# Decay attention and a softplus MLP on one core: another operation for the weights' sign, chunk 1's attention events one slot later, and the last weight sums spread over three steps

## The chip, the cores and the metric

The kernel runs on one core of one Trainium2 chip. The metric is device time in microseconds (us) of one execution. TensorE (PE in the profile) does the matmuls, VectorE (DVE), ScalarE (ACT) and GpSimd (POOL) the elementwise work, and SyncE (SP) issues most transfers; ACT issues some.

## The reference

The inputs are q, k, v of shape 4 x 8 x 768 x 64 (batch, heads, positions, dims), a decay per head, and two weight matrices `w_in` (512 x 2048) and `w_out` (2048 x 512), which come as float64. Cut to what matters:

```python
for b in range(nb):                      # 12 blocks of 64 positions
    intra = einsum('bhic,bhjc->bhij', qb, kb) * Dmask        # lam ** (i - j), causal
    out[block] = einsum('bhij,bhjd->bhid', intra, vb) + einsum('bhid,bhde->bhie', qb * lam_pow, kv_state)
    kv_state = lam ** 64 * kv_state + einsum('bhsd,bhse->bhde', kb * rev_pow, vb)
x = out as (4 * 768, 512)
h = x @ w_in
g = maximum(h, 0) + log1p(exp(-abs(h)))  # softplus
return (g @ w_out).astype(float32)
```

## The kernel before

**Chunks, units, slots.** The 768 positions are six chunks of 128. In each chunk the eight heads form four pairs, so there are 24 attention *units* g = 4 x chunk + pair. The MLP works on one chunk of all four batches at a time: 512 columns of x, 16 slices f of the hidden layer. Chunks 0 and 1 (`STD = 2`) take one *slot* s per slice, s = 4 to 31: `mlp1(s)` makes h in 12 matmuls, `chain_act`, `chain_hi`, `chain_lo` (named after their slot) make softplus and its two parts, and `mlp2(s)`, four slots later (`LAG`), adds 12 matmuls to the four output banks. Every value is split in a high and a low part in TensorE's number format, and three of the four products are taken. Chunks 2 to 5 go in two groups of two by a Strassen-like scheme with seven block products P1 to P7 per pair of slices (`product`); there a *step* i does two slices. The loop over steps stands once for chunks 2 and 3 (`more` true) and once for chunks 4 and 5.

**Weights.** `wts` holds the raw words of the float64 weights. `w_scale` (ACT) scales the high word as if it were a float, into `c`; `w_round` (ACT) rounds the low word to its top three bits, in place; `w_shift` (DVE) shifts `c` left by 3; `w_sign` (DVE) puts in the sign; `w_add` (DVE, an exact integer add) adds the low word; `w_hi` (ACT) and `w_lo` (DVE) split the result. In the first slots this goes block by block in an order written out by hand; from slot 4 on a group of two blocks is loaded into one tile `raws`, scaled, shifted and added in one slot (`new`) and split in the next (`old`). The converted blocks are written to DRAM (`store_blocks`) and read back later (`load_w1`, `load_w2`). `block_sums`, `store_sums` and `send_sums` make the block sums that the scheme needs, split them (a copy on ACT, then a subtraction on DVE) and send them to DRAM; sums 0 to 6 are made in slots 18 to 31, sums 7 in the steps.

**Attention beside the MLP.** Unit g needs `k_decay` (ACT), `q_decay` (DVE), scores (`mm_scores`, into banks x and y), `mask_scores` and `update_states` (DVE), and a slot later or more `mm_out`, whose result is copied to `xr` (`x_raw`). `event(g)` does `mm_out` of unit g - 1, then scores, mask, copy and states of unit g. `both_at` says in which slot each event stands; `k_decay` and `q_decay` are issued at the start of the slot before (`units_at`). Events 9 to 16 lie in slots 16, 18, ..., 30, between two `mlp2` of one slot; the slot after has no `mlp2`. Units 17 and up have their event in the steps. In the last slots `x_sums_early` and `x_sums_late` prepare the inputs of P1 to P7 from `xr`: the early ones of half 0 in slot 29, the late ones of half 0 in slot 30, the early ones of half 1 in slot 31, the late ones of half 1 behind it, just ahead of the steps.

**Order and storage.** Each engine works in program order (`manual_schedule`). A transfer waits in SP's queue until its buffer is free, and those behind it wait too. Large tiles share 21 buffers (`t8`), conversion and g tiles seven (`t4`), attention tiles five (`t2`). Of the eight PSUM banks four hold outputs (`obank`), two are the work tile `t` (`work`), and two (`bank`) are taken in turn by h, by the scores x and y of an event, and in the steps by a and c.

Of the kernel before, what the change touches and what calls it, by code (L numbers as in the profile page):

```python
# [7 lines left out]
F32 = mybir.dt.float32  # L8
F32R = mybir.dt.float32r
U32 = mybir.dt.uint32  # L10
AF = mybir.ActivationFunctionType
ALU = mybir.AluOpType
PSUM = bass.MemoryType.PSUM
# [5 lines left out]
NP = H // 2  # L19
# [3 lines left out]
NF = DFF // 128  # L23
LAG = 4
# [8 lines left out]
def decay_attention_softplus_ffn(  # L33
# [7 lines left out]
    nc = tc.nc  # L41
# [168 lines left out]
    def raw_at(ks, word):  # L210
        i = ks[0] % 2
        return raws[ks[0]][:, i : i + len(ks), :, word]
# [12 lines left out]
        nc.vector.tensor_single_scalar(out=c, in_=c, scalar=3, op=ALU.logical_shift_left)  # L225

    def w_sign(*ks):
        c = conv[ks[0]]
        nc.vector.scalar_tensor_tensor(  # L229
            out=c, in0=raw_at(ks, 1), scalar=0x80000000, in1=c, op0=ALU.bitwise_and, op1=ALU.bitwise_or  # L230
        )

    def w_add(*ks):
# [196 lines left out]
    def mlp2(ss):  # L430
        c = ss[0] // NF
        ends = ss[-1] % NF == NF - 1
        if ss[0] % NF == 0:
            o_tiles[c] = [obank(f"o{c}_{b}") for b in range(B)]
        if ends:
            ob = t8([128, B, 512], F32, f"ob{c}")
        for b in range(B):
            for s in ss:
                f = s % NF
                g, w = g_tiles[s], w_second(s)  # L440
                for n, (i, j) in enumerate(((0, 0), (0, 1), (1, 0))):
                    nc.tensor.matmul(  # L442
                        o_tiles[c][b], lhsT=g[:, i, b * 128 : (b + 1) * 128], rhs=w[:, j],
                        start=f == 0 and n == 0, stop=f == NF - 1 and n == 2,
                    )
            if ends:
                copy = nc.vector.tensor_copy if b % 2 else nc.scalar.copy
                copy(out=ob[:, b], in_=o_tiles[c][b])
                queue = nc.scalar if c == NCH - 1 and b % 2 == 0 else nc.sync
                queue.dma_start(out=out[b * S + c * C : b * S + (c + 1) * C, :], in_=ob[:, b])  # L450
# [147 lines left out]
    def low_of(g, l):  # L598
        nc.vector.tensor_sub(out=g[:, 1], in0=l, in1=g[:, 0])  # L599
# [37 lines left out]
    last = STD * NF  # L637
    scores_at = {3 * n + 3: NP + n for n in range(NP)}
    outs_at = {s + 2: g for s, g in scores_at.items()}
    scores_at[NF - 1] = 2 * NP  # L640
    both_at = {2 * g - 2: g for g in range(2 * NP + 1, 4 * NP + 1)}
    units_at = {**scores_at, **both_at}

    def event(g):
# [12 lines left out]
    for s in range(LAG, last):  # L657
        if s + 1 in units_at:
            k_decay(units_at[s + 1])
            q_decay(units_at[s + 1])  # L660
        chain_act(s - 1)
        chain_hi(s - 1)
        chain_lo(s - 1)
        old, new = w_group(s - 1), w_group(s)
        if old:
            w_hi(*old)
        if new:
            w_scale(*new)
            w_round(*new)
        if old:  # L670
            w_lo(*old)
        if new:
            w_shift(*new)
            w_sign(*new)
            w_add(*new)
        if s - 1 not in both_at:
            mlp2([s - LAG])
        if s in scores_at:
            scores_of(scores_at[s])
            if scores_at[s] == 2 * NP:  # L680
                keep_values(2 * NP)
        if s in both_at:
            event(both_at[s])
            mlp2([s + 1 - LAG])
        if s in outs_at:
            g = outs_at[s]
            w = work(f"z{g}")
            mm_out(g, w)
            x_high(g, w)
            x_low(g, w)  # L690
        mlp1(s)
        w_load(2 * s + (8 if s < 9 else 6))
        if s in units_at and s < NF - 2:
            load_upto(units_at[s] + 2)
        if s >= NF - 2 and s % 2 == 0:
            load_upto(2 * NP + 2 + (s - NF + 2) // 2 + (s >= NF))
        if s > NF and s % 2 == 0:
            load_w2((s - NF) // 2)
        if s > NF + 2 and s % 2 == 0:
            send_sums((s - NF) // 2 - 2)  # L700
        if 8 <= s < 8 + NF:
            store_blocks(s - 8)
        if s > NF and s % 2 == 0:
            block_sums((s - NF) // 2 - 1)
        if s > NF + 2 and s % 2:
            store_sums((s - NF - 1) // 2 - 1)
        for at, name, n in ((23, "P1", 0), (23, "P1", 1), (25, "P2", 0), (25, "P2", 1)):
            if s == at:
                x_block(name, xr[2][:, n + (2 if name == "P2" else 0)], n)
        if s == last - 3:  # L710
            x_sums_early(2, 0)
        if s == last - 2:
            x_sums_late(2, 0)
            load_w1(0)
        if s == last - 1:
            x_sums_early(2, 1)
# [14 lines left out]
    for c in range(STD, NCH, 2):  # L731
        more = c + 2 < NCH
        lb = {}
        gs = {}
        for i in range(NF // 2):
            if more and i == 1:
                block_sums(NF // 2 - 1)
                store_sums(NF // 2 - 1)
                send_sums(NF // 2 - 1)
            unit = nxt if more else None  # L740
            if unit is not None:
                load_upto(unit + 2)
            if i + 1 < NF // 2:
                load_w1(i + 1)
            load_w2(i)
            if unit is not None and unit < NG:
                k_decay(unit)
                q_decay(unit)
            if i % 2 == 0:
                l4 = t8([128, 4, 512], F32, f"lb{c}_{i}")  # L750
            for n in range(2):
                lb[2 * i + n] = l4[:, 2 * (i % 2) + n]
            ta, tb = t4([128, 2, 512], F32, f"ta{c}_{i}"), t4([128, 2, 512], F32, f"tb{c}_{i}")
            p1, u2, u3, c21 = ta[:, 0], ta[:, 1], tb[:, 0], tb[:, 1]
            a, b_ = bank(f"a{c}_{i}"), work(f"b{c}_{i}")[:, 0]
            product("P1", i, a)
            nc.scalar.copy(out=p1, in_=a)  # L757
            product("P6", i, b_)
            nc.vector.tensor_add(out=u2, in0=b_, in1=p1)  # L759
            c_ = bank(f"c{c}_{i}")  # L760
            product("P5", i, c_)
            product("P2", i, a, False)
            la = tl([128, 512], F32, f"la{c}_{i}")
            nc.scalar.activation(la, a, AF.Softplus)  # L764
            ga = parts_of(f"g{c}_{2 * i}", la)
            product("P7", i, b_, False)
            nc.vector.tensor_add(out=u3, in0=b_, in1=p1)  # L767
            nc.vector.tensor_add(out=u3, in0=c_, in1=u3)
            nc.scalar.activation(lb[2 * i + 1], u3, AF.Softplus)
            low_of(ga, la)  # L770
            run(rest, 2)
            product("P4", i, b_, False)
            nc.vector.tensor_add(out=c21, in0=b_, in1=p1)
            nc.scalar.activation(c21, c21, AF.Softplus)
            gb = parts_of(f"g{c}_{2 * i + 1}", c21)
            product("P3", i, c_, False)
            nc.vector.tensor_add(out=u2, in0=c_, in1=u2)
            nc.scalar.activation(lb[2 * i], u2, AF.Softplus)
            run(rest, 4)
            if unit is not None and unit <= NG:  # L780
                event(unit)
                nxt += 1
            low_of(gb, c21)
            run(rest)
            pair = [(2 * i + n, (ga, gb)[n], w2_tiles[i][:, n]) for n in range(2)]
            rest = seconds(c, pair, i == NF // 2 - 1)
        ahead = 2
        def split(f):
            gs[f] = parts_of(f"g{c + 1}_{f}", lb[f])
            low_of(gs[f], lb[f])  # L790
        for f in range(ahead):
            split(f)
        for i in range(2):
            load_w2(i)
        run(rest)
        xc.clear()
        steps = []
        if more:
            steps = [lambda n=n, m=m: x_block(n, xr[c + 2][:, m + (2 if n == "P2" else 0)], m) for n in ("P1", "P2") for m in range(2)]
            for n in range(2):  # L800
                steps += [lambda n=n: x_sums_early(c + 2, n), lambda n=n: x_sums_late(c + 2, n)]
        for f in range(NF - 2):
            if f % 2 == 0 and f // 2 + 2 < NF // 2:
                load_w2(f // 2 + 2)
            if f + ahead < NF:
                split(f + ahead)
            if f >= 1:
                run(steps, 1)
            if f == 9 and more:
                load_w1(0)  # L810
            run(seconds(c + 1, [(f, gs.pop(f), w2_tiles[f // 2][:, f % 2])]))
        rest = seconds(c + 1, [(f, gs[f], w2_tiles[f // 2][:, f % 2]) for f in (NF - 2, NF - 1)], True)
# [41 lines left out]
```

## Time and profile before

| | |
|---|---|
| time, median of 3 | 597.03 us (596.62 to 598.16) |
| profiled execution, time | 595.9 us |
| profiled execution, span | 594.1 us |
| PE busy | 576.5 us, 97% of the span |
| DVE busy | 321.6 us, 54% |
| ACT busy | 256.8 us, 43% |
| granted TensorE clock | 0.999 |

A row of the views by line gives line, engine, operation, the tiles written and read, count, then busy time, mean ns of one, and the idle time of the engine just ahead. A row of the timeline gives start, duration, engine, line, operation, and in brackets the idle time ahead and what ended it. A row of the view by stretches gives the busy time of PE, PE's weight loads, DVE, ACT and POOL, each with its number of instructions, the granted clock, the busy share of the DMA engines and the GB/s.

### The profile page before, as it was taken

The numbers are of one execution on the slowest core, as the hardware profiler recorded it, in microseconds if no ns is written. First come the engines' busy times: TensorE is split into PE (matmuls) and PEld (weight loads), VectorE is DVE, ScalarE is ACT, GpSimd is POOL, SyncE is SP. The second block draws the span as 40 slices with busy tenths as digits, with TensorE's granted clock in tenths as the row PEclk, the third lists the DMA queues.
The fourth block names the chain that finished last, engine by engine and source line by source line (L and its number), as shares of the span: only waits on it lengthen the run. The fifth ranks groups of instructions, "written<-read, shape, count | busy, mean of one in ns | idle before, by whom it ended". The sixth has DMA issues, their size and how long they took to land.

```text
span 594.1 us, 12014 instructions
## 1 busy us (share of the span) xinstructions
PE 576.5 (97%) x5203; PEld 469.4 (79%) x5203; DVE 321.6 (54%) x492; ACT 256.8 (43%) x416; POOL 4.1 (1%) x11
## 2 busy tenths in 40 slices
PE   8899989989999999989999999999999999999997
PEld 6677778768888888778888888888888888888886
DVE  7779998974767768664543443295133333333410
ACT  3777776663345434543333332463142222224310
POOL 2000000000000000000000000000000000000000
PEclk9999999999999999999999999999999999999999
DMA  8997565883999974649965647489267454473101
GB/s 292 407 407 272 186 202 178 273 298 114 327 399 387 412 285 172 253 159 386 413 257 188 237 171 271 155 315 375 88 237 294 167 190 140 137 288 121 56 1 71
DMA packets 38452, 142.34 MB, mean 240 GB/s; under 512 B 3712, under 2 KB 5760, under 8 KB 31360
## 3 DMA queue, kind: packets, MB, share of 16 engines
q1 hardware_dynamic: 35808, 136.86, 62.7%
q10 hardware_dynamic: 2592, 4.72, 2.1%
q8 instruction: 41, 0.67, 0.5%
q14 instruction: 11, 0.09, 0.0%
HBM read 112.20 MB, written 29.36 MB: 238 GB/s over the span
## 4 chain that ended last, share of the span: by engine, by line
PE 76%; DVE 10%; DMA 8%; ACT 2%; issue 1%; SPq 1%; DVEq 0%; ACTq 0%
PE o L607 30%; PE b L588 11%; PE h L421 8%; PE o L442 8%; PE c L588 7%; PE a L588 7%; DMA att<-in_att 4%; DMA g<-w 3%; PE x L311 2%; PE z L326 2%; DVE c L235 2%; DVE st L343 2%; DMA raw<-in_wts 1%; DVE w L242 1%; DVE c L229 1%
## 5 line engine op out<-in xcount | busy, mean ns | idle before, releaser
L607 PE MATMUL o<-w,g 128*128 128x512 f32 x816 | 192.7, 390 | 0.0
L607 PEld LDWEIGHTS o<-w,g 128*128 128x128 f32 x816 | 152.5, 188 | 31.9
L421 PE MATMUL h<-x,w 128*128 128x512 f32 x384 | 94.4, 395 | 2.1 <-DVE w L242 2.1
L421 PEld LDWEIGHTS h<-x,w 128*128 128x128 f32 x384 | 70.9, 188 | 19.9 <-DVE w L242 3.7
L442 PE MATMUL o<-w,g 128*128 128x512 f32 x336 | 82.3, 393 | 1.1 <-DVE w L242 0.8
L442 PEld LDWEIGHTS o<-w,g 128*128 128x128 f32 x336 | 62.3, 188 | 15.1 <-DVE w L242 1.2
L588 PE MATMUL a<-xcP,w1a 128*128 128x512 f32 x192 | 49.0, 391 | 1.5 <-ACT ta L757 1.5
L588 PE MATMUL b<-xcP,w1b 128*128 128x512 f32 x192 | 48.8, 389 | 0.0
L759 DVE TENSOR_TENSOR ta<-b,ta 128x512 f32<-128x512 f32 x16 | 11.0, 690 | 60.9 <-PE b L588 60.9
L588 PEld LDWEIGHTS a<-xcP,w1a 128*128 128x128 f32 x192 | 35.9, 188 | 9.8 <-ACT ta L757 2.3
L588 PEld LDWEIGHTS b<-xcP,w1b 128*128 128x128 f32 x192 | 36.0, 188 | 7.5
L402 ACT ACTIVATE l<-h 128x512 f32<-128x512 f32 x32 | 19.0, 595 | 49.1 <-PE h L421 46.5
L599 DVE TENSOR_TENSOR g<-lb,g 128x512 fp32r<-128x512 f32 x32 | 21.1, 688 | 34.1 <-ACT g L595 34.1
L767 DVE TENSOR_TENSOR tb<-b,ta 128x512 f32<-128x512 f32 x16 | 11.1, 691 | 50.4 <-PE b L588 50.4
L338 DVE TENSOR_TENSOR a<-x,mask 128x512 f32<-128x512 f32 x15 | 10.4, 691 | 44.1 <-PE y L313 23.4
L410 DVE TENSOR_TENSOR g<-l,g 128x512 fp32r<-128x512 f32 x32 | 22.1, 690 | 18.8 <-ACT g L406 18.7
L764 ACT ACTIVATE la<-a 128x512 f32<-128x512 f32 x16 | 9.6, 598 | 52.3 <-PE a L588 52.3
L757 ACT COPY ta<-a 128x512 f32<-128x512 f32 x16 | 9.3, 584 | 51.8 <-PE a L588 51.8
L595 ACT CAST g<-lb 128x512 fp32r<-128x512 f32 x32 | 18.7, 619 | 18.4 <-PE o L607 17.6
L588 PE MATMUL b<-xcP,w1a 128*128 128x512 f32 x96 | 24.9, 391 | 0.8 <-DVE xcP L561 0.4
L326 PEld LDWEIGHTS z<-qd,st 64*64 64x64 f32 x640 | 17.0, 134 | 10.0 <-issue 9.7
L386 ACT COPY xr<-z 128x512 f32<-128x512 f32 x16 | 9.4, 585 | 36.0 <-PE z L330 35.5
(100 smaller groups left out, 774.4 us busy)
## 6 DMA issues: line engine op xcount, KB each, us to landing
w<-g SPq DMA_DIRECT2D x39, 1024.0 KB, 5.6
att<-in_att SPq DMA_DIRECT2D x48, 512.0 KB, 10.0
raw<-in_wts SPq DMA_DIRECT2D x32, 512.0 KB, 10.2
w1a<-g SPq DMA_DIRECT2D x16, 1024.0 KB, 6.8
g<-w SPq DMA_DIRECT2D x24, 512.0 KB, 9.3
w1b<-g SPq DMA_DIRECT2D x16, 768.0 KB, 6.7
g<-parts SPq DMA_DIRECT2D x16, 512.0 KB, 9.0
out_dram<-ob ACTq DMA_DIRECT2D x18, 256.0 KB, 2.0
```

Source lines behind the costliest of these rows:

```text
L235: nc.vector.tensor_add(out=c, in0=c, in1=raw_at(ks, 0))
L311: nc.tensor.matmul(x[r, cols], lhsT=k[r, b, t], rhs=q[r, b, t], start=True, stop=True)
L326: nc.tensor.matmul(w[half(t), s, cols], lhsT=st[r, b, t], rhs=qd[r, b, t], start=True, stop=False)
L343: nc.vector.scalar_tensor_tensor(out=to[:, :, t], in0=of[:, :, t], scalar=lam_c[r, h : h + 1], in1=u[:, :, t], op0=ALU.mult, op1=ALU.add,)
L402: nc.scalar.activation(l_tiles[s], h_tiles.pop(s), AF.Softplus)
L410: nc.vector.tensor_sub(out=g[:, 1, :], in0=l_tiles.pop(s), in1=g[:, 0, :])
L421: nc.tensor.matmul(h_tiles[s], lhsT=w[:, i, cs], rhs=x[:, j, :], start=p == 0 and n == 0, stop=p == NP - 1 and n == 2,)
L442: nc.tensor.matmul(o_tiles[c][b], lhsT=g[:, i, b * 128 : (b + 1) * 128], rhs=w[:, j], start=f == 0 and n == 0, stop=f == NF - 1 and n == 2,)
L588: nc.tensor.matmul(to, lhsT=w[:, k, n, p * 128 : (p + 1) * 128], rhs=x[:, j, p], start=start and p == 0 and m == 0, stop=p == 1 and m == 2 ...
L595: nc.scalar.copy(out=g[:, 0], in_=l)
L599: nc.vector.tensor_sub(out=g[:, 1], in0=l, in1=g[:, 0])
L607: nc.tensor.matmul(outs[c, b], lhsT=g[:, i, b * 128 : (b + 1) * 128], rhs=w[:, j], start=f == 0 and n == 0, stop=f == NF - 1 and n == 2,)
```

## The change

Three places. `w_sign` no longer masks the sign out of the raw high word and joins it to `c`; it takes the 16-bit half that holds the sign, masks it, and writes it over the upper half of the rounded low word of the same tile, so that the add that follows brings it in. Events 9 to 16 move to slots 17, 19, ..., 31, with `k_decay` and `q_decay` of their units a slot later too; the second `mlp2` of slot 31 is left to `old_seconds`, which did slots 28 and 29 before and still does. Sums 7, made, split and sent at the start of step 1 of chunks 2 and 3, are now made at the end of step 0, split at the end of step 1 and sent at the end of step 2.

```diff
     def w_sign(*ks):
-        c = conv[ks[0]]
-        nc.vector.scalar_tensor_tensor(
-            out=c, in0=raw_at(ks, 1), scalar=0x80000000, in1=c, op0=ALU.bitwise_and, op1=ALU.bitwise_or
+
+        k, n = ks[0], len(ks)
+        halves = raws[k].rearrange("q n m t -> q n (m t)").bitcast(U16).rearrange("q n (m t) -> q n m t", t=4)
+        i = k % 2
+        nc.vector.tensor_single_scalar(
+            out=halves[:, i : i + n, :, 1], in_=halves[:, i : i + n, :, 3], scalar=0x8000, op=ALU.bitwise_and
         )
...
-    both_at = {2 * g - 2: g for g in range(2 * NP + 1, 4 * NP + 1)}
+    both_at = {2 * g - 1: g for g in range(2 * NP + 1, 4 * NP + 1)}
...
         if s in both_at:
             event(both_at[s])
-            mlp2([s + 1 - LAG])
+            if s < last - 1:
+                mlp2([s + 1 - LAG])
...
-            if more and i == 1:
-                block_sums(NF // 2 - 1)
-                store_sums(NF // 2 - 1)
-                send_sums(NF // 2 - 1)
...
             low_of(gb, c21)
+            if more and i == 0:
+                block_sums(NF // 2 - 1)
+            if more and i == 1:
+                store_sums(NF // 2 - 1)
+            if more and i == 2:
+                send_sums(NF // 2 - 1)
             run(rest)
```

More of the change, by code (lines that the diff above doesn't have):

```diff
@@ L10 @@
 U32 = mybir.dt.uint32
+U16 = mybir.dt.uint16
 AF = mybir.ActivationFunctionType
```

## The prediction

> **What bounds the kernel now.** I read the page's busy table first, then busy time by stretches, then TensorE's (PE's) rows with the idle time ahead of each.
>
> ```profile
> PE 576.5 (97%) x5203; PEld 469.4 (79%) x5203; DVE 321.6 (54%) x492; ACT 256.8 (43%) x416; POOL 4.1 (1%) x11
> ...
> 35.00:125.00 90.00, 86.77 (x899) 68.29 (x898) 80.23 (x101) 64.85 (x87) 0.00 (x0) 1.00 0.71 247
> 125.00:215.00 90.00, 87.06 (x1211) 72.17 (x1210) 60.41 (x106) 38.31 (x67) 0.00 (x0) 1.00 0.89 327
> 215.00:245.00 30.00, 29.20 (x245) 23.25 (x244) 24.65 (x42) 14.79 (x25) 0.00 (x0) 1.00 0.63 236
> 245.00:265.00 20.00, 18.49 (x200) 14.98 (x199) 11.65 (x20) 10.24 (x18) 0.00 (x0) 1.00 0.34 129
> 265.00:594.10 329.10, 325.49 (x2139) 269.14 (x2137) 119.87 (x187) 108.62 (x186) 0.00 (x0) 1.00 0.56 208
> ```
>
> PE is the bound: 576.5 of 594.1 us. The change takes no matmul away, so it can only win PE's idle time: 3.2 us at 35 to 125 (where VectorE, DVE, is busy 80 of 90), 2.9 at 125 to 215, 0.8 at 215 to 245, 1.5 at 245 to 265. The 3.6 us at the end lie behind the last matmul, which the change does not touch. These rows say what PE waited for:
>
> ```profile
> 49.10 0.50 PE L442 MATMUL o<-w,g 128*128 128x512 f32 x1 [0.34 <-ACT w L238]
> 50.36 2.79 PE L442 MATMUL o<-w,g 128*128 128x512 f32 x11 [0.76 <-DVE w L242]
> ...
> 74.55 2.79 PE L421 MATMUL h<-x,w 128*128 128x512 f32 x11 [0.57 <-DVE w L242]
> 88.39 2.79 PE L421 MATMUL h<-x,w 128*128 128x512 f32 x11 [1.34 <-DVE w L242]
> 114.55 2.79 PE L421 MATMUL h<-x,w 128*128 128x512 f32 x11 [0.17 <-DVE w L242]
> ...
> 129.81 0.34 PE L326 MATMUL z<-qd,st 64*64 64x64 f32 x8 [2.94 <-DVE st L343]
> ...
> 240.36 0.73 PE L588 MATMUL b<-xcP,w1a 128*128 128x512 f32 x2 [0.38 <-ACT xcP L560]
> 241.51 0.50 PE L588 MATMUL b<-xcP,w1a 128*128 128x512 f32 x1 [0.42 <-DVE xcP L561]
> ...
> 262.45 1.65 PE L588 MATMUL a<-xcP,w1a 128*128 128x512 f32 x6 [1.51 <-ACT ta L757]
> ```
>
> The first five are converted weights that come late, 3.2 us; then one event's states, 2.9; then the first Strassen block sum, 0.8; then step 1's copy of P1, 1.5. Each part of the change bears on one of these.
>
> **Part 1, the sign.** What the operations cost now:
>
> ```profile
> L229 DVE SCALAR_TENSOR_TENSOR c<-raw,c 128x1024 uint32<-128x1024 uint32 x13 | 15.9, 1226 | 0.5
> L229 DVE SCALAR_TENSOR_TENSOR c<-raw,c 128x512 uint32<-128x512 uint32 x6 | 4.1, 690 | 0.1
> L225 DVE TENSOR_SCALAR c<-c 128x1024 uint32<-128x1024 uint32 x13 | 8.9, 686 | 0.0
> L225 DVE TENSOR_SCALAR c<-c 128x512 uint32<-128x512 uint32 x6 | 3.1, 511 | 0.5 <-ACT c L217 0.4
> ```
>
> The old sign (L229) reads two tensors: 1226 ns for a pair of weight blocks, 690 for one. The new one reads one tensor, writes it in place and has as many elements. Its nearest row is the shift (L225), also one tensor with a constant: 686 and 511. But the shift's words lie side by side, the sign's 2-byte halves 8 bytes apart, as L229 reads raw. So the ends are 0.69 and 1.23 for a pair, and an in-place write of every fourth half could cost more than 1.23 (a rival below). I take 0.69, since the count of tensors is what sets the two rows apart: saved are 13 x 0.54 + 6 x 0.18 = 8.1 us of DVE. [...]
>
> Of the 8.1 us only what PE waited for counts, and the new sign adds a wait. The old one read c, which the shift had written; the new one overwrites half of the low word, so it waits for ScalarE's (ACT's) round (L221). Around the longest stall:
>
> ```profile
> 77.38 0.60 ACT L402 ACTIVATE l<-h 128x512 f32<-128x512 f32 x1 [1.57 <-PE h L421]
> ...
> 80.54 1.15 ACT L221 ACTIVATE raw<-raw 128x1024 uint32<-128x1024 uint32 x1
> ...
> 80.76 0.69 DVE L225 TENSOR_SCALAR c<-c 128x1024 uint32<-128x1024 uint32 x1
> 81.48 1.23 DVE L229 SCALAR_TENSOR_TENSOR c<-raw,c 128x1024 uint32<-128x1024 uint32 x1
> 82.84 1.22 DVE L235 CUSTOM_DVE_ANT_0 c<-raw,c 128x2048 uint16<-128x2048 uint16 x1
> ...
> 87.11 1.22 DVE L242 TENSOR_TENSOR w<-c,w 128x1024 fp32r<-128x1024 f32 x1
> ```
>
> The round ends at 81.69, so here the sign starts 0.25 later than now, ends at 82.44 and saves 0.27, not 0.54. And this chain starts afresh at PE's own h (ACT waited 1.57 for it): nothing saved before 77.38 shortens it. Of the 1.34 at 88.39 I give back 0.27. Behind the waiting sign stand the add, then what that slot has next on DVE (mask, states, next g); all move with it and end no later than now. At 49 to 50 us the chain runs back without such a restart over two single signs and one pair: 0.18 + 0.18 + 0.54 = 0.90 of 1.10. Before 74.55 DVE runs without a gap over 0.3 from 49 on, through four pair signs at 0.27 to 0.54, 1.1 or more: the 0.57 goes, and so do the 0.17 at 114.55 and the last 0.05 of the 3.23. Sum: 0.27 + 0.90 + 0.79 = **2.0 us**; ends 0 and 3.2.
>
> **Part 2a, the first event.** 2.94 us at 129.81:
>
> ```profile
> 119.77 0.91 ACT L289 ACTIVATE kd<-att,rp 128x256 f32<-128x256 f32 x2 [3.95 <-DMA att<-in_att]
> ...
> 121.84 0.69 DVE L410 TENSOR_TENSOR g<-l,g 128x512 fp32r<-128x512 f32 x1 [2.92 <-ACT g L406]
> ...
> 127.88 1.79 DVE L343 SCALAR_TENSOR_TENSOR st<-st,lam_c,w 64x256 f32<-64x256 f32 x4
> ```
>
> In slot 15 ACT's first work is unit 9's k_decay, which waits 3.95 us for that unit's load. The slot's softplus stands behind it, DVE's g behind that (2.92 idle), and the states (127.88) that mm_out(8) of event 9 reads. With events at odd slots, k_decay and q_decay of unit 9 go to slot 16, behind a load that landed before 119.8, and mm_out(8) to slot 17, two matmul blocks (5.4 us) later. The states then end near 125 and are read after 132. Next late would be mlp1(16): its weights and x are long in SBUF. **2.9 us**; ends 2 and 2.9. The later events keep their order on PE with one slot's offset; attention loads sit in the queue where they sat, and by the order of releases each finds a buffer freed earlier, though units are held 6.6 us longer. Chunk 0's output DMAs fall behind slot 18's loads on SP instead of ahead of them; nothing is loaded late by that.
>
> **Part 2b, the last event** costs time. Slot 30 now holds x_sums_late(2, 0) in front of event 16, and slot 31 has no mlp2 behind it:
>
> ```profile
> 210.89 3.02 PE L442 MATMUL o<-w,g 128*128 128x512 f32 x12
> ...
> 219.19 2.88 PE L442 MATMUL o<-w,g 128*128 128x512 f32 x12
> ...
> 224.05 3.02 PE L442 MATMUL o<-w,g 128*128 128x512 f32 x12
> ...
> 224.15 0.69 DVE L338 TENSOR_TENSOR a<-x,mask 128x512 f32<-128x512 f32 x1 [0.90 <-PE y L313]
> ...
> 226.70 1.29 DVE L518 TENSOR_TENSOR full<-w 128x512 f32<-128x512 f32 x2
> ...
> 229.50 0.68 DVE L575 TENSOR_TENSOR tt<-xr,tt 128x512 f32<-128x512 f32 x1
> ...
> 230.21 1.82 ACT L560 CAST xcP<-tt 128x512 fp32r<-128x512 f32 x3 [5.88 <-DVE tt L575]
> ...
> 232.47 0.59 ACT L402 ACTIVATE l<-h 128x512 f32<-128x512 f32 x1
> ```
>
> Count from event 15's end on PE (210.89 is the row behind it). A block of 12 takes 2.7, an event 2.2. After the change PE does mlp2(26), mlp1(29) (done 5.5), mlp1(30) (8.2), mlp2(27), mm_out(15) (12.1), and scores of unit 16. x16 and y16 take the two h banks; y16's was h30's, free once chain_act(30) has read it. ACT has that read behind x_sums_late's four copies. Their time: h29 done 5.5; softplus, cast and low part 2.0; block_sums 2.8 (226.70 to 229.50); then 3.6 from L575's start to the softplus's end (229.50 to 233.06): 14.0. So the scores start at 14.1 instead of 12.1 and end at 15.2; the mask (0.69) frees x16's bank at about 16.0, and mlp1(31), which takes that bank and follows at once, starts then and not at 13.3: a stall of **2.7 us**. In exchange P6's sums come in time: now 17.4 us pass from the mask (224.15) to the low part that ends the wait (241.51); 2.8 of block_sums and 3.6 of x_sums_late(2, 0) then lie ahead of the mask, so 11.0 are left, from 15.3 to 26.3, and PE, 2.7 later than now, wants that part at about 26.8 (three blocks of 2.7 and one and a half products of 1.4 after 16.0). The 0.8 at 240 us goes. Net **-1.9 us**; ends 0 (the bank comes free in time, P6 waits as now) and -4.
>
> **Part 3, the last sums.** Step 1 now:
>
> ```profile
> 260.07 1.05 ACT L531 CAST parts<-sums 128x1024 fp32r<-128x1024 f32 x1 [2.58 <-DVE sums L526]
> 261.03 0.90 ACT L289 ACTIVATE kd<-att,rp 128x256 f32<-128x256 f32 x2
> 261.83 0.56 ACT L757 COPY ta<-a 128x512 f32<-128x512 f32 x1
> ```
>
> ACT stands at the parts copy until DVE's sums end, k_decay and P1's copy stand behind it, and P2 waits 1.51. With store_sums at step 1's end ACT goes straight to k_decay and P1's copy is done before 260.9, when P2 is due. block_sums keeps its place on DVE. The moved copy (1.05) and its low part (L242's size, 1.22) lie behind event 18, under the rest's 2.7 us and three products; uncovered they would cost 1.05. On SP step 1's four loads no longer stand behind send_sums(7), which goes out in step 2 and is read in step 6. **1.5 us**; ends 1.0 and 1.5.
>
> **Sum.** 2.0 + 2.9 - 1.9 + 1.5 = 4.5 us against the profiled execution's 595.9: 591.4. That execution is 1.1 below the median of 597.0, so for the median **592.5**.
>
> **Rivals.**
> (a) No stall at slot 31, because scores or mask come earlier than worked out; P6 then still waits 0.7. 592.5 - 2.7 + 0.7 = 590.5. For it: DVE idles at several places there; against: the bank order follows from the code.
> (b) The stalls of 35 to 125 us re-form: behind each saved sign stands a chain that begins at PE's h, as at 77.38. Part 1 gives 0.5: 594.0.
> (c) The sign does not get faster (1.23): part 1 gives nothing and the wait for the round adds some 0.5: 595.0.
> (d) Slower than before: the scattered 2-byte writes make the sign of a pair d us, with d well over 1.23. Eleven pairs lie between 44 and 124 us; with DVE at 80 of 90, each adds up to d - 1.23 to PE's waits. The other parts give 2.5, so it decides from d = 1.5 if nothing absorbs it, and from 1.9 if half of DVE's 9.8 idle us do. At 2.3 us the time is about 602. Nothing in the profile shows such a write; L229's reads at 8-byte steps cost what unit steps cost.
>
> **How the numbers follow.** Chances: forecast 0.52, (a) 0.18, (b) 0.12, (c) 0.11, (d) 0.07. A measurement of this kernel tells about 0.3%, 1.8 us, from no change: faster is below 595.2. Forecast, (a), (b) and half of (c): 0.86 faster; the rest of (c) and a little of (d) 0.08; slower 0.06. The range 589.5 to 595.5 takes in (a), (b), (c) and the ends of parts 1 and 2b; it leaves out (d).
>
> **What would show it.** L229 as a TENSOR_SCALAR of 0.69 us for 1024 elements; no wait over 0.3 at 49, 74 and 114 us, and one near 1.1 at 86; no wait for states near 127; a new wait of mlp1(31) or of y's scores near 220, 2 to 3 us, with no wait for xcP behind it; no wait for ta at step 1. Wrong: a sign of 1.2 us or more, or more than 4 us lost around slot 31.

## The result, and the profile after

| | before | after |
|---|---|---|
| median of 20 runs | 597.01 us (594.99 to 598.38) | 593.12 us (592.52 to 596.09) |
| ratio, 95% interval | | 0.9945 (0.9933 to 0.9957) |
| profiled execution: time, span | 595.9, 594.1 us | 593.05, 591.2 us |
| end of the last matmul in the trace | 590.48 us | 587.65 us |

The change makes the kernel 0.55% faster: 3.9 us by the medians, 2.9 by the profiled executions. The forecast was 592.5. But the sign did not get cheaper, and the gain stands on the other two parts and on something that the forecast left out. First the busy table and the stretches of after. The columns are those of the rows shown of before.

```profile
PE 576.2 (97%) x5203; PEld 470.4 (80%) x5203; DVE 321.7 (54%) x492; ACT 256.7 (43%) x416; POOL 4.1 (1%) x11
```

```profile
0.00:35.00 35.00, 30.28 (x520) 22.12 (x520) 25.02 (x39) 20.25 (x37) 4.12 (x11) 1.00 0.95 359
35.00:125.00 90.00, 85.88 (x895) 67.82 (x895) 82.58 (x102) 65.05 (x87) 0.00 (x0) 1.00 0.71 247
125.00:215.00 90.00, 90.00 (x1224) 74.58 (x1224) 58.69 (x107) 39.06 (x67) 0.00 (x0) 1.00 0.93 340
215.00:245.00 30.00, 27.41 (x239) 22.58 (x238) 23.98 (x41) 14.44 (x27) 0.00 (x0) 1.00 0.63 235
245.00:265.00 20.00, 20.00 (x208) 16.59 (x207) 12.41 (x22) 9.38 (x17) 0.00 (x0) 1.00 0.90 336
265.00:591.20 326.20, 322.65 (x2126) 266.76 (x2124) 119.03 (x185) 108.56 (x185) 0.00 (x0) 1.00 0.53 194
```

PE's idle time, stretch minus its first busy column, before to after: 3.23 to 4.12 us in 35 to 125, 2.94 to 0 in 125 to 215, 0.80 to 2.59 in 215 to 245, 1.51 to 0 in 245 to 265, 3.61 to 3.55 behind. Those five together are 1.83 us less. In the first 35 us PE idles 4.72 us now; before it was 5.51 (594.1 less 576.5 busy, less the other five), 0.79 less. With 0.3 us less of busy time that makes the 2.9 us of the spans. PE's rows with a wait of 0.15 us or more, from 40 us on (the count at the end is that of the matmuls in the row; in brackets the idle time ahead and what ended it; three of 0.76, 0.34 and 0.15 left out):

```profile
48.71 0.50 PE L446 MATMUL o<-w,g 128*128 128x512 f32 x1 [0.23 <-ACT w L242]
...
74.82 2.78 PE L425 MATMUL h<-x,w 128*128 128x512 f32 x11 [0.74 <-DVE w L246]
88.90 2.81 PE L425 MATMUL h<-x,w 128*128 128x512 f32 x11 [1.60 <-DVE w L246]
115.22 2.79 PE L425 MATMUL h<-x,w 128*128 128x512 f32 x11 [0.31 <-DVE w L246]
228.07 0.27 PE L317 MATMUL y<-att,kd 64*64 64x64 f32 x1 [1.76 <-ACT l L406]
230.04 3.02 PE L425 MATMUL h<-x,w 128*128 128x512 f32 x12 [0.82 <-DVE a L342]
```

The converted weights come later than before at three places (0.57 to 0.74, 1.34 to 1.60, 0.17 to 0.31), the wait for states at 129.81 is gone, P6's waits for `xcP` and P2's for `ta` are gone, and two new waits of 1.76 and 0.82 us stand around slot 31. The sign and the shift of after by line and shape (busy us, mean ns of one, idle time of DVE just ahead):

```profile
L233 DVE TENSOR_SCALAR raw<-raw 128x1024 uint16<-128x1024 uint16 x13 | 17.4, 1336 | 2.5 <-ACT raw L222 2.5
...
L226 DVE TENSOR_SCALAR c<-c 128x1024 uint32<-128x1024 uint32 x13 | 8.9, 687 | 0.0
L233 DVE TENSOR_SCALAR raw<-raw 128x512 uint16<-128x512 uint16 x6 | 4.5, 746 | 0.0
```

The one-tensor sign takes 1336 ns for a pair of blocks where the two-tensor one took 1226, and DVE now waits 2.5 us in all for ACT's round. In the chain of the longest stall:

```profile
81.02 0.69 DVE L226 TENSOR_SCALAR c<-c 128x1024 uint32<-128x1024 uint32 x1
81.99 1.33 DVE L233 TENSOR_SCALAR raw<-raw 128x1024 uint16<-128x1024 uint16 x1 [0.28 <-ACT raw L222]
```

The sign starts 0.28 us behind the shift's end and ends at 83.32; in before it ended at 82.71, with the shift 0.26 earlier.

### The profile page after: what moved, and what is told of

Same layout as the page of the kernel before. It is cut to its first block, busy times and chain, and to the rows that moved or that the text cites. A ratio compares the mean times of both kernels' runs of the same rounds, so it can differ in the third digit from the quotient of the medians.

```text
span 591.2 us, 12000 instructions
## 1 busy us (share of the span) xinstructions
PE 576.2 (97%) x5203; PEld 470.4 (80%) x5203; DVE 321.7 (54%) x492; ACT 256.7 (43%) x416; POOL 4.1 (1%) x11
## 3 DMA queue, kind: packets, MB, share of 16 engines
q10 hardware_dynamic: 2592, 4.72, 2.1%
## 4 chain that ended last, share of the span: by engine, by line
PE 79%; DVE 9%; DMA 6%; ACT 3%; issue 2%; SPq 1%; ACTq 0%
PE o L611 32%; PE b L592 11%; PE h L425 8%; PE o L446 8%; PE a L592 7%; PE c L592 7%; DMA att<-in_att 4%; DVE raw L233 2%; DVE c L239 2%; PE x L315 2%; PE z L330 2%; DVE st L347 1%; DMA raw<-in_wts 1%; PE z L334 1%; DMA g<-w 1%
## 5 line engine op out<-in xcount | busy, mean ns | idle before, releaser
L592 PE MATMUL c<-xcP,w1a 128*128 128x512 f32 x96 | 24.4, 389 | 0.0
```

Source lines behind the costliest of these rows:

```text
L592: nc.tensor.matmul(to, lhsT=w[:, k, n, p * 128 : (p + 1) * 128], rhs=x[:, j, p], start=start and p == 0 and m == 0, stop=p == 1 and m == 2 ...
```

## The experiments

Theory after the result: the sign costs time because its 2-byte halves are written at 8-byte steps, and the two schedule moves carry the gain. Rivals: the sign's chain was misjudged (a cheaper sign would not have helped), or the moves and the sign act on each other. The first four kernels split the change.

**Parts 2 and 3 with the old sign.** After, with

```diff
-            out=halves[:, i : i + n, :, 1], in_=halves[:, i : i + n, :, 3], scalar=0x8000, op=ALU.bitwise_and
+            out=c, in0=raw_at(ks, 1), scalar=0x80000000, in1=c, op0=ALU.bitwise_and, op1=ALU.bitwise_or
```

> The changed kernel with the sign operation of before (two tensors, 1.23 us a pair) and the other two parts kept. Theory: the new sign costs time, 1.34 us a pair against 1.23 and a wait for the round of about 0.28 at most of the slots; PE idle at 35 to 125 us went from 3.2 to 4.1, so this kernel is 0.7 to 0.9 us faster than the changed one (a profiled span near 590.4) and 3.9 to 4.7 us faster than before. Rival: the new sign is neutral or a gain and the 0.9 belongs to other parts; then the span stays at 591.2 or rises.

Measured: 592.89 us, ratio 0.9941 (0.9924 to 0.9958), span 590.5. The converted weights are waited for as before (0.35, 0.77, 0.57, 1.34, 0.16 us), and the two waits at 227 to 230 us stay (1.76, 0.83). So part 1 brings nothing: it costs 0.7 us by the profiled spans and 0.85 by the medians of the runs at full clock (0.999 or more: 592.02 here, 592.87 in after). By the medians of all runs it is 0.2, which is inside the intervals.

**The new sign alone.** Before, with the new `w_sign`.

> The kernel before with the new sign alone. Theory: 0.7 to 0.9 us slower than before, PE idle at 35 to 125 us about 4.1 in place of 3.2, the waits of 2.94, 0.8 and 1.51 us unchanged. The prediction's part 1, with a sign of 0.69 us: 2.0 us faster.

Measured: 599.18 us, ratio 1.0039 (1.0024 to 1.0054). The sign by itself makes the kernel slower. Its profile shows the weights' waits of after (0.68, 1.58, 0.32) and the old ones of the other parts (2.99, 0.35, 0.42, 1.52). The waits for weights alone do not make the 2.4 us between the medians. In this profile the granted clock fell near the end of the 2.99 us wait. Its stretches, clock third from the right:

```profile
125.00:128.00 3.00, 2.26 (x10) 1.53 (x9) 2.88 (x3) 1.95 (x5) 0.00 (x0) 1.00 0.69 194
128.00:131.00 3.00, 0.75 (x28) 0.78 (x32) 2.90 (x7) 0.76 (x1) 0.00 (x0) 0.84 1.05 322
131.00:134.00 3.00, 3.00 (x113) 2.93 (x106) 1.13 (x2) 1.70 (x4) 0.00 (x0) 0.59 0.96 335
134.00:137.00 3.00, 3.00 (x14) 2.45 (x14) 2.90 (x6) 0.21 (x1) 0.00 (x0) 1.00 1.04 387
```

The 0.16 and 0.41 that lack, of 3 us each, are 1.71 us of work, or, as an estimate, 3.4 us at a clock of 0.50, which before shows for 592.90 to 594.08, behind its last matmul. Its two runs at full clock took 597.47 and 597.79, those of before 594.9 to 596.2. Some 2 us remain between them, of which the waits in 35 to 125 us explain 0.8 (4.0 instead of 3.2). By the profiles another 1.1 lies behind the last matmul: from there to the end of the span pass 4.75 us (592.45 to 597.2), 3.62 in before, because the end of the program waits 2.6 us for the last output transfer instead of 1.4. The half sign and the two kernels with the word sign below end the same way; why is not shown.

**The events alone**, and **the sums alone**: before, with the `both_at` and `mlp2` hunks, and before, with the hunks of the steps.

> The kernel before with the events one slot later alone. Theory: the 2.94 us wait for states at 130 us and the 0.8 for P6's sums go, a wait of 2.6 us at the last event comes (scores wait for ACT's softplus of h30, then mlp1(31) for the mask); net 1.2 to 1.5 us faster than before. Rival: the events' move gives nothing by itself and the gain at 130 us came from the sign; then no change.

> The kernel before with the last sums at the ends of steps 0 to 2 alone. Theory: the 1.51 us wait of P2 for the copy ta at 262 us goes and nothing takes its place: 1.5 to 1.7 us faster. Rival: the moved copy and its low part push step 2's P2 by up to 1.05 us: 0.5 us faster.

Measured: events 594.05 us, ratio 0.9964 (0.9950 to 0.9978); sums 595.09, ratio 0.9977 (0.9966 to 0.9988). In the events kernel the 2.94 us wait and P6's 0.8 are gone, 1.77 and 0.82 stand at 227 to 230, and P2's wait stays (1.47). In the sums kernel only P2's wait is gone. Each part does what it did in after, alone. The events gain 2.69 us by the medians, more than the 1.2 to 1.5 expected; the runs at full clock, 593.55 and 594.05 here and 595.23 to 595.47 in before, lie some 1.6 apart, and the rest goes with falls of the clock, to which the filled wait below returns. With the old sign's 592.89 the two gains nearly add: 2.69 and 1.65 make 4.34, and 3.85 was measured with both.

**What of the sign is slow.** After, with groups of four single masks of 128x1024 elements behind the work, each on a tile that nothing else uses; the time of this kernel is not compared.

```diff
+    for _ in range(4):
+        nc.vector.tensor_single_scalar(out=hw[:, :, :, 1], in_=hw[:, :, :, 3], scalar=0x8000, op=ALU.bitwise_and)
+    for _ in range(4):
+        nc.vector.tensor_single_scalar(out=pt[:, :, :, 0], in_=pt[:, :, :, 1], scalar=0x8000, op=ALU.bitwise_and)
...
```

> The changed kernel with one-tensor bit masks of 2 x 512 elements added behind the end, four of each form, beside no transfer and no other engine: (1) the sign as it is, in place, 2-byte halves at 8-byte steps; (2) 4-byte words at 8-byte steps; (3) as 1, but into another tile; (4) halves at 8-byte steps into side-by-side halves; (5) side-by-side into 8-byte steps; (6) halves at 4-byte steps, another tile; (7) side by side both. Theory step: 8-byte steps alone cost the shift's rate, so 1, 2 and 3 take 1.2 to 1.35 us, 6 is nearer 0.69, 7 below 0.69. Theory width: 2-byte access is what costs, 2 takes 0.69, 1, 3 and 6 take 1.34. Theory in place: 1 and 2 take 1.34, 3 takes 0.69. Theory traffic: other transfers slowed the sign; all forms here take 0.69 or less. The prediction's step (tensors read set the price): 1 takes 0.69.

By line and shape, in the order 2-byte halves written at 8-byte steps (L841 from dense halves, L837 from another tile at 8-byte steps, L833 in place), written at 4-byte steps (L843), 4-byte words in place at 8-byte steps (L835), halves read at 8-byte steps and written dense (L839), all dense (L845):

```profile
L841 DVE TENSOR_SCALAR probe_a<-probe_b 128x1024 uint16<-128x1024 uint16 x4 | 5.2, 1300 | 0.1
L837 DVE TENSOR_SCALAR probe_b<-probe_a 128x1024 uint16<-128x1024 uint16 x4 | 5.2, 1298 | 0.1
L833 DVE TENSOR_SCALAR probe_a<-probe_a 128x1024 uint16<-128x1024 uint16 x4 | 5.1, 1283 | 0.1
L843 DVE TENSOR_SCALAR probe_b<-probe_a 128x1024 uint16<-128x1024 uint16 x4 | 2.9, 735 | 0.1
L835 DVE TENSOR_SCALAR probe_a<-probe_a 128x1024 uint32<-128x1024 uint32 x4 | 2.8, 695 | 0.1
L839 DVE TENSOR_SCALAR probe_b<-probe_a 128x1024 uint16<-128x1024 uint16 x4 | 2.8, 694 | 0.1
L845 DVE TENSOR_SCALAR probe_b<-probe_a 128x1024 uint16<-128x1024 uint16 x4 | 1.7, 426 | 0.1
```

Halves read at 8-byte steps and written dense take 694, against 426 all dense; whole words at that step take 695, against 687 for the shift's dense words; in place it is 1283, into another tile 1298. The three rows of 1283 to 1300 are those that write 2 bytes at 8-byte steps, from dense halves too (1300). At 4-byte steps it is 735. So neither the step nor the width gives that price by itself, as two of the expected theories had it; here it took both, and on the side of the write.

**A sign at the price that was forecast.** Before, with the new sign on 256 of the 512 columns; the weights of the other columns get no sign.

```diff
+            out=halves[:, i : i + n, 0:256, 1], in_=halves[:, i : i + n, 0:256, 3], scalar=0x8000, op=ALU.bitwise_and
```

> The kernel before with the new sign on half of the columns only (256 of 512; the other half of the weights keeps a positive sign), so the operation is about 0.75 us a pair, near the price that the prediction took. It tests the rest of the prediction's part 1. Theory: with that price the waits of PE at 35 to 125 us fall from 3.2 to about 1.2 us, the one of 1.34 staying near 1.1 as it starts at PE's own h; 1.5 to 2.0 us faster than before. Rival: a shorter sign gives nothing, since ACT's round and PE's h set the chain everywhere; waits stay near 3 us and the time does not move.

Measured: 595.21 us, ratio 0.9971 (0.9956 to 0.9986); the sign takes 754 ns a pair and still waits 2.5 us for the round. PE's waits here and a little behind:

```profile
85.18 2.79 PE L425 MATMUL h<-x,w 128*128 128x512 f32 x11 [1.01 <-DVE w L246]
...
120.90 2.81 PE L446 MATMUL o<-w,g 128*128 128x512 f32 x11 [0.23 <-DVE w L246]
126.30 0.34 PE L330 MATMUL z<-qd,st 64*64 64x64 f32 x8 [2.58 <-DVE st L347]
```

No wait over 0.1 is left at 49 and none at 74; at 85 stands 1.01, where the forecast left 1.07 (1.34 less 0.27). In the whole stretch PE idles 2.62 us, of which 1.28 belong to the wait for states that now begins ahead of 125; the 1.34 that are left compare with the 1.2 of the forecast. The chain of part 1 was worked out right; only the price of the instruction was wrong.

**The first event's wait without moving the events.** Before, with unit 9's decays issued in slot 16 instead of 15:

```diff
-        if s + 1 in units_at:
+        if s + 1 in units_at and s + 1 != NF:
...
+        if s == NF:
+            k_decay(units_at[s])
+            q_decay(units_at[s])
```

> The kernel before with k_decay and q_decay of unit 9 issued at the start of slot 16 instead of slot 15, all events where they were. Theory: the 2.94 us wait at 130 us comes only from ACT standing at unit 9's load in slot 15, so it goes without any event's move; waits of 0.8 and 1.5 us at 240 and 262 us stay, and no wait comes at slot 31: 2.9 to 3.2 us faster than before, more than with all events moved. Rival: mm_out(8) in slot 16 is too early for the states in any case, 1 us or more of the wait stays.

Measured: 592.43 us, ratio 0.9927 (0.9908 to 0.9945), span 590.4. The 2.94 us wait is gone, nothing appears at slot 31, P6 and P2 wait as before (0.38, 0.42, 1.52). ACT starts the slot's softplus at 116.61, when PE's h is there, and not at 120.58 behind the load. These four lines alone do as well as the whole change: the cause was ACT standing at unit 9's load, and the later slots of all eight events were not needed. By the medians they gain 4.3 us, more than the 2.9 to 3.2 expected; by the runs at full clock 3.3 (592.39 against 595.66).

**The second `mlp2` of slot 31 kept.** After, with

```diff
-            if s < last - 1:
-                mlp2([s + 1 - LAG])
+            mlp2([s + 1 - LAG])
...
-    run(old_seconds([last - 4, last - 3]))
+    run(old_seconds([last - 3]))
```

> The changed kernel with mlp2(28) left in slot 31 behind the last event, and old_seconds doing slot 29 alone. Theory: of the new waits at 227 to 231 us the second (0.82, mlp1(31) for the mask) goes, since mlp2(28) lies between; the first (1.76, scores for ACT's softplus of h30) stays: 0.8 to 1.0 us faster than the changed kernel, span near 590.3. Rival: both waits have one cause, DVE's work in slots 30 and 31, and the second only moves to P6's sums: no change.

Measured: 591.95 us, ratio 0.9919 (0.9900 to 0.9938), span 590.2. Of the two new waits one is left:

```profile
227.84 0.27 PE L317 MATMUL y<-att,kd 64*64 64x64 f32 x1 [1.77 <-ACT l L406]
```

So the 0.82 us was the cover that the moved `mlp2` took away. The 1.76 stays; ACT's rows, shown further below, put it down to `x_sums_late` in front of the softplus, and no run here moves `x_sums_late` to test that.

**A sign on whole words.** Before, with ACT's round writing its result as 16 bits into the high word's lower half, and the sign masking that word in place:

```diff
-        nc.scalar.activation(raw_at(ks, 0), raw_at(ks, 0), AF.Copy, scale=2.0**-29)
+        nc.scalar.activation(halves[:, i : i + n, :, 2], raw_at(ks, 0), AF.Copy, scale=2.0**-29)
...
-            out=c, in0=raw_at(ks, 1), scalar=0x80000000, in1=c, op0=ALU.bitwise_and, op1=ALU.bitwise_or
+            out=raw_at(ks, 1), in_=raw_at(ks, 1), scalar=0x8000FFFF, op=ALU.bitwise_and
```

> The kernel before with the sign as a one-tensor operation on whole 4-byte words: ACT's round writes its result (0 to 8) into the lower 16 bits of the high word, the sign operation keeps the sign bit and those 16 bits of that word in place, and the add takes that word. Theory (2-byte writes at 8-byte steps are what made the sign 1.34 us): the sign takes 0.69 us a pair, PE's waits at 35 to 125 us fall from 3.2 to 1.1 or so as with the half sign, 2.5 to 3.0 us faster than before. Rival: ACT's round now makes such 2-byte writes and gets slower by 0.1 to 0.6 us a pair, and the sign waits for it longer; the gain is 1 us or less.

Measured: 606.45 us, ratio 1.0154 (1.0125 to 1.0183): the rival, and by more than it said. By line and shape:

```profile
L224 ACT ACTIVATE raw<-raw 128x1024 uint16<-128x1024 uint32 x13 | 32.9, 2529 | 0.5
...
L231 DVE TENSOR_SCALAR raw<-raw 128x1024 uint32<-128x1024 uint32 x13 | 9.0, 694 | 16.3 <-ACT raw L224 16.3
```

DVE's sign is now at the 0.69 us of the forecast, but it waits 16.3 us for ACT: the round of a pair takes 2529 ns with the 2-byte result at 8-byte steps, against 1142 in before with a 4-byte result at the same steps. So a 2-byte write at 8-byte steps was the slower one on ACT too.

**All waits at once, with that sign.** The kernel just above, with unit 9's decays in slot 16, the sums at the ends of steps 0 to 2, and `store_sums(6)`, `send_sums(6)` behind `x_sums_late(2, 1)`.

> A version from what the runs showed, on the kernel before: the word sign, unit 9's decays in slot 16, events where they were, the last sums at the ends of steps 0 to 2, and store_sums(6) and send_sums(6) behind x_sums_late(2, 1). Theory: of PE's waits behind 35 us only one near 1.0 at 85 us is left; by the waits 2.2 + 2.9 + 0.8 + 1.5 = 7.4 us and some 0.2 us for each restart, span near 586, and no stretch of half clock since no wait reaches 2 us: 8 to 9.5 us faster than the median of before. Rival: the gains do not add up, since an earlier PE meets weights and sums later; 5 to 6 us.

Measured: 601.11 us, ratio 1.0067 (1.0045 to 1.0088). The sign's ACT time spoils it (waits of 2.08, 2.68 and 1.31 us before 140). P6's waits are gone, but P2 of step 0 waits 0.78 for `ta`: with the copy and its DMAs right behind `x_sums_late`, they only moved the wait on. Two of these waits also cost clock: one of 2.08 us ends at 62.62, one of 2.68 at 93.87, and behind each the clock falls, where no fall was expected. That no wait under 2 us brings a fall was the expectation's own assumption, and no run shows it: 9 of the 20 runs of after have a fall, and the longest wait of PE in after's profile, from 40 us on, is 1.76. Around the first (clock third from the right):

```profile
60.00:63.00 3.00, 0.92 (x27) 0.50 (x29) 2.96 (x4) 2.52 (x5) 0.00 (x0) 1.00 1.01 389
63.00:66.00 3.00, 3.00 (x61) 2.43 (x50) 1.90 (x3) 2.91 (x3) 0.00 (x0) 0.57 0.85 203
66.00:69.00 3.00, 3.00 (x13) 2.42 (x12) 2.23 (x3) 1.34 (x3) 0.00 (x0) 0.86 0.94 303
```

**The long wait filled.** Before, with ten matmuls ahead of event 9 into a bank that nothing reads:

```diff
+            if s == NF:
+                fill, wf = bank("fill"), w_of(0, 0)
+                for _ in range(10):
+                    nc.tensor.matmul(fill, lhsT=wf[:, 0, :128], rhs=wf[:, 0, :], start=True, stop=True)
```

> The kernel before with ten matmuls of converted weights into a bank that nobody reads put ahead of event 9, where PE waits 2.9 us; their 2.3 us fit into the wait. Theory: the runs of before lose 1.7 us in most executions because this wait lets the granted clock fall to 0.5 for 3.41 us; with PE kept active the clock stays at 1.0 in nearly all runs, the states still end when they did, and the median is 1.0 to 1.5 us below that of before, its best runs equal to those of before. Rival: the fall has nothing to do with the wait; clocks of 0.997 stay as frequent and the time is that of before or longer.

Measured: 595.25 us, ratio 0.9977 (0.9966 to 0.9988), with no useful work saved. A mean clock of 0.997 is counted here as one fall of 1.71 us (of 595), 0.994 as two: this kernel's profile, at 0.997, has 0.63 in 31 to 34 us and 0.80 in 34 to 37, which is 1.71 lost, and the one of all waits at once, at 0.994, has two falls. Of the 12 runs 8 were at 0.999 or more and none under 0.997; of the 16 runs of before in the same job 5, and 6 at 0.993 or 0.994. Before's runs at full clock took 595.22 to 596.15, these 594.89 to 595.67. So the gain, 1.5 us by the medians, goes with fewer falls of the clock. That the clock would stay at 1.0 in nearly all runs did not come true, and the falls do not all come from that wait: the one in this kernel's profile, at 31 us, lies far ahead of it, and 9 of the 20 runs of after have one or more though after has no such wait. Nor does every fall cost 1.7 us: two of the four runs at 0.997 here took 595.20 and 595.23, as long as those at full clock.

**The best version.** Before, with the old sign and the events where they were, the edit of the decays above, the sums at the ends of steps 0 to 2, and

```diff
-    send_sums(NF // 2 - 2)
...
+            if more and i == 0:
+                store_sums(NF // 2 - 2)
+                send_sums(NF // 2 - 2)
+                block_sums(NF // 2 - 1)
```

(`store_sums(6)` is taken out of slot 31).

> The kernel before (old sign, chunk 1's events where they were) with three moves alone: unit 9's decays at the start of slot 16 instead of slot 15 (the 2.94 us at 129.81), the last sums at the ends of steps 0 to 2 (the 1.51 at 262.45), and the parts copy, low part and DMAs of block sums 6 from slot 31 to the end of step 0, which takes 1.05 us of ACT and 1.23 us of DVE from ahead of P6's sums (the 0.38 and 0.42 at 240 and 241). Theory that PE's waits are each one late producer, that these add, and that without the 2.9 us wait the granted clock falls less often: no wait for states near 127, none for xcP at P6, none for ta in step 1, the 3.2 us at 35 to 125 unchanged; last matmul end 5.2 us earlier than 590.5, span about 588.9; median 590.5, ratio 0.989, below the 592.9 of the changed kernel with the old sign, 0.994. Rival, that what is taken from one place is paid at the next: P6's wait only moves on to P2 of step 0, which waits 0.7 for ta, since ACT has unit 17's decays ahead of that copy; 591.3, ratio 0.9905. Rival, that moves of ACT's work into step 0 hold up its softplus of step 1: waits of PE over 0.5 us at 255 to 265, 592 or more.

Measured: 589.57 us, ratio 0.9893 (0.9873 to 0.9914), span 587.7. Its stretches:

```profile
35.00:125.00 90.00, 86.78 (x900) 68.63 (x899) 82.64 (x103) 66.03 (x89) 0.00 (x0) 1.00 0.71 248
125.00:215.00 90.00, 90.00 (x1224) 74.63 (x1223) 60.02 (x108) 38.58 (x67) 0.00 (x0) 1.00 0.91 339
215.00:245.00 30.00, 30.00 (x251) 24.68 (x250) 23.50 (x40) 14.01 (x26) 0.00 (x0) 1.00 0.52 194
245.00:265.00 20.00, 19.86 (x206) 16.11 (x205) 12.27 (x21) 11.02 (x19) 0.00 (x0) 1.00 0.68 250
```

From 125 to 265 us PE idles 0.14 instead of 5.25, and the weights' 3.2 are the only waits left between 35 us and the last matmul. The span is 6.4 us shorter, 1.2 more than foretold: PE's busy time is also 1.2 less (575.3). That may be the restart behind each of the four waits that went (an estimate from before's rows: a matmul alone behind a wait shows 0.50 us, and rows of 11 and of 12 take 2.79 and 3.02, 0.23 for one more). If so, it is that of the three waits for `xcP` and `ta`: in the kernel with unit 9's decays alone, whose last matmul ends 3.68 us ahead of before's, an earlier start (0.77) and shorter waits (2.91) account for all of it.

## Why the prediction was right, and where it was not

The time came out, 593.1 against 592.5, but not all the terms did, and that it came so near is in part luck: the sign's term was off by 2.9 us, and 2.1 of that were made up by things for which the forecast had no term.

- **Part 1, the sign: wrong.** Forecast +2.0 us, measured -0.9 in that stretch (3.23 to 4.12 idle). The step that failed is the price: "I take 0.69, since the count of tensors is what sets the two rows apart". The probe shows that the write sets it: 1283 to 1300 ns for 2 bytes at 8-byte steps, 694 when only the read has that step. The prediction's own list of what would show it wrong began with "a sign of 1.2 us or more", and that is what came. L229 had only shown reads at that step; the sentence with rival (d) said that no row showed such a write, and still the low end was taken. Rival (c) came nearest in size (1.23 and some 0.5 for the round, so 0.5 lost), and (d)'s mechanism was there at d = 1.34, below the 1.5 from which it would decide. The rest of the step held: the wait for the round is 0.28 in the longest stall's chain (0.25 forecast), and the half sign left 1.01 of the 1.34 (1.07). Compared with before, that wait is more of the loss at this stall than the price, 1.33 against 1.23.
- **Part 2a: right.** 2.9 forecast, 2.94 gone; unit 9's decays do not stall ACT in slot 16, and the decays alone show the cause.
- **Part 2b: right.** Forecast 2.7 for the last event, measured 1.76 + 0.82 = 2.58. The forecast counted from event 15's end, which is 213.94 in after: y's scores were to start 14.1 us behind it and `mlp1(31)` 16.0, and they start at 228.07 and 230.04, 14.13 and 16.10 behind it. Its text calls the whole 2.7 a stall of `mlp1(31)`, though by its own times 2.0 of it are the scores' late start, and it put the place near 220 us. P6's 0.8 went, as forecast, though without the margin that was written: 16.0, three blocks of 2.7 and one and a half products of 1.4 make 26.2, not 26.8, so that by its own numbers the low part at 26.3 is 0.1 late; after shows no wait there. ACT's rows of after:

```profile
225.18 1.82 ACT L564 CAST xcP<-tt 128x512 fp32r<-128x512 f32 x3 [4.16 <-DVE tt L579]
226.91 0.61 ACT L564 CAST xcP<-xr 128x512 fp32r<-128x512 f32 x1
227.43 0.59 ACT L406 ACTIVATE l<-h 128x512 f32<-128x512 f32 x1
```

  The four copies stand ahead of the softplus that PE waits for, and ACT idled 4.16 us in front of them.
- **Part 3: right.** 1.5 forecast, 1.51 gone, by itself as well.
- **Sum.** Forecast 4.5 us of the profiled execution, measured 2.85. By idle time: 0.9 lost, 2.94 won, 1.79 lost, 1.51 won, 1.8 in all, where the same four terms were to give 4.5. The other 1.1 had no term. Some 0.3 of it is the start: PE's block of 15 `mlp1` matmuls starts at 31.64 in before, 31.36 in after and 31.31 with the old sign, so this is not the sign. Up to there PE idles 0.8 us less and is busy 0.5 longer. The other 0.8 is PE's busy time behind that point; it may be the restarts behind the waits that went, as in the best version, and no run settles it.
- **From the profiled execution to the median: a term that was missing.** The step "that execution is 1.1 below the median, so for the median 592.5" took the distance as fixed. Before's median lies above its profiled execution because most runs have a fall of the clock: of 52 runs 16 at full clock (median 595.5), and by the mean clock 25 with one fall (596.8) and 11 with two (597.5). Of after's 20 runs 11 are at full clock (592.9). After, without the wait of 2.9 us, had fewer falls, and its median lies 0.07 above its profiled execution. This gives back 1.03 us of the 1.65 that the sum lacks, and the forecast came within 0.6 by errors of both signs.

## What to carry to other kernels

Price an operation by a row with the same write pattern, element size and step of the output included; a row that only reads that way told nothing about it here (694 ns for the read of halves at 8-byte steps, 1283 to 1300 for the write). When an engine waits for a late operand, look first for the one instruction in front of the producer that stands at a load, and move that alone: four lines did here what the whole change did, with no new wait. Here a wait of the matmul engine at which its clock fell cost up to 1.7 us more than its length (the stretches of the sign alone), and since the fall came in some executions only (36 of 52 runs of before, 9 of 20 of after), it showed in the median more than in one profile.

## What the runs showed of the hardware

- Writing 2 bytes at 8-byte steps was slow on two engines: on DVE 1.28 to 1.30 us for 128x1024, against 0.70 for 4-byte words at those steps, 0.74 for 2 bytes at 4-byte steps and 0.43 all dense (the probe); on ACT 2.53 us (the word sign) against 1.14 for 4-byte words at the same steps (before). Other steps were not tried on ACT.
- The granted clock fell in some executions of the same kernel and not in others. Where the stretches show a fall, they lack 1.71 us each time: 0.16 and 0.41 of 3 us in the sign alone, 0.43 and 0.14 in all waits at once, 0.37 and 0.20 in the filled wait; by the estimate above 3.4 us at 0.50. In the profiles it fell at or behind waits of 2.99 us (the sign alone), 2.84 (the sums alone), 2.08 and 2.68 (all waits at once), 2.68 and 3.89 (the word sign); it did not fall behind 2.94 (before), 2.58 (the half sign) and one of 2.13 (the word sign), so the length alone does not decide. For the sums alone and the word sign this is read from PE's rows: behind 2.84 and 3.89 the groups of eight `z` matmuls follow each other by 0.21 us, behind 2.94 by 0.12, and behind the word sign's 2.68 ten `h` matmuls take 3.63 us, behind its 2.13 eleven take 2.79. What else decides is not shown.
